# Decode attention on one core: K and V in rows of 64 KiB, four heads in a transfer, three slots

## The chip, the cores and the metric

The kernel runs on 1 core of one Trainium2 chip. The metric is device time in microseconds (us) of that core, as the median of the executions of one kernel.

## The reference

Four sequences decode one token each. Attention with 32 heads reads a cache of 8192 positions; a small feed-forward block reads the same normed input; both are added to x.

```python
B, Sq, D, H, Sk, Dh, F = 4, 1, 512, 32, 8192, 128, 1792      # all bf16
xn = layernorm(x)
q  = (xn @ wq) -> (B, H, 1, Dh)
p  = softmax(q . k_cache * Dh ** -0.5)
o  = p . v_cache
out = x + o.reshape(B, Sq, H*Dh) @ wo + (silu(xn @ w_gate) * (xn @ w_up)) @ w_down
```

K and V are 268 MB each. Everything else is 14 MB: the whole question is how fast 551 MB come in, and whether the work on them hides beneath.

## The kernel before

One tile is two heads of one sequence: 4 MiB of K or of V, on 128 partitions with 32 KiB each, so one DMA row is 32 KiB. Five slots of this size take K and V in turn.

```python
HT = 2                      # heads in a tile
NT = 64                     # tiles
NSLOT = 5; LP = 2           # slots; P*V runs two tiles behind

def t_piece(n, g):          # VectorE: one eighth of a K tile, transposed in pairs of d
    kt = kt_pool.tile([P, TG * Dh], bf16)                      # 5 buffers
    nc.vector.transpose(out=kt..., in_=k_tiles[n][:, g*w:(g+1)*w])   # 128 x 1024 uint32

def s_piece(n, g):          # TensorE: its scores, 4 matmuls
    for jp in range(4):
        mm(s_ps[gr], zq[gr % 2][:, bb, jp, off:off+P], kt[:, jp//2, :, jp%2])

for i in range(NT + LP):
    load_k(i + 2); load_v(i)
    for g in range(8):
        t_piece(i, g); s_piece(i, g)
        if g == 0 and bb == 0: pt_turn(gr - 1)   # VectorE: turns P of the group of two tiles, 2 transposes
    ...                                          # every second tile: maximum, exp (ScalarE), new q
    for k in range(32): pv_chunk(i - LP, k)      # TensorE: P*V of an earlier tile
    row_sums(...)                                # matmul, then VectorE's reciprocal
```
(The set-up, the feed-forward block, the finish of the output and the product with wo are cut.)

## Time and profile before

| | before |
|---|---|
| median (4 runs beside the changed kernel) | 1289.14 us, 1288.77 to 1289.36 |
| span of the profiled run | 1287.1 us |
| last packet of V landed | 1282.4 us |
| VectorE's instructions | 951 |

The lines that show what bounds it stand in the prediction. Here are five more from the page: the busy time of the engines (us, share of the span, number of instructions), two small rows of the list of DMA queues (packets, MB, share of the 16 engines' time), the chain that ended last (followed back from the last instruction), by engine, and the group of the large transposes.

```profile
PE 1083.1 (84%) x4778; PEld 430.3 (33%) x4778; DVE 738.1 (57%) x951; ACT 39.7 (3%) x87; POOL 5.3 (0%) x13
...
q8 instruction: 37, 0.61, 0.2%
q14 instruction: 12, 0.10, 0.0%
...
DMA 50%; PE 31%; DVE 14%; issue 5%; ACT 1%; SPq 0%; DVEq 0%
...
L277 DVE STREAM_TRANSPOSE kt<-slot 128x1024 uint32<-128x1024 uint32 x512 | 587.6, 1210 | 90.4 <-DMA slot<-in_A_k_cache_dram 89.5
```

Half of the chain is DMA: the transfers set the end. The rows q8 and q14, 49 packets with 0.7 MB out of 551, are the engines' instruction fetches.

### The profile page before, as it was taken

The page shows a single profiled execution, that of the slowest core. Times are in us where ns is not written, and L with a number is a line of the kernel's source. Part 1 is how long each engine was busy: PE and PEld are TensorE (multiplying, and loading weights), DVE is VectorE, ACT ScalarE, POOL GpSimd, SP SyncE. Part 2 cuts the span into 40 slices and gives each one's busy share as a digit, 9 for nine tenths or more (in the row PEclk, how much of TensorE's full clock was granted, in tenths as well). Part 3 has the DMA queues.
Part 4 walks back from the last instruction along what each step waited for, and adds up shares of the span by engine and source line. Part 5 has one row for each costly group of instructions (what it writes and reads, how often), then busy time and mean ns, then how long its engine had stood idle before and what let it go on. Part 6 is the DMA issues. An engine that isn't in the chain of part 4 may idle for free.

```text
span 1287.1 us, 11189 instructions
## 1 busy us (share of the span) xinstructions
PE 1083.1 (84%) x4778; PEld 430.3 (33%) x4778; DVE 738.1 (57%) x951; ACT 39.7 (3%) x87; POOL 5.3 (0%) x13
## 2 busy tenths in 40 slices
PE   4888888888888798897997888888887988978788
PEld 1334333333333333332333333333333333333334
DVE  6663556546556556466556566465465465573544
ACT  1000000000000000000000000000000000000000
POOL 1000000000000000000000000000000000000000
PEclk9898898998989999898998989989899898989899
DMA  9999999999999999999999999999999999999997
GB/s 407 427 430 435 437 425 437 429 436 431 432 435 428 436 432 433 431 432 435 431 435 428 434 432 431 436 431 433 430 434 431 437 430 432 433 431 427 433 434 304
DMA packets 21529, 551.49 MB, mean 428 GB/s; under 512 B 2268, under 2 KB 2792, under 8 KB 3944
## 3 DMA queue, kind: packets, MB, share of 16 engines
q1 hardware_dynamic: 21464, 550.78, 99.4%
q8 instruction: 37, 0.61, 0.2%
q14 instruction: 12, 0.10, 0.0%
q10 hardware_dynamic: 16, 0.01, 0.0%
HBM read 550.77 MB, written 0.00 MB: 428 GB/s over the span
## 4 chain that ended last, share of the span: by engine, by line
DMA 50%; PE 31%; DVE 14%; issue 5%; ACT 1%; SPq 0%; DVEq 0%
DMA slot<-in_A_k_cache_dram 44%; PE oacc L76 17%; PE sps L76 12%; DVE kt L277 11%; DMA slot<-in_A_v_cache_dram 6%; PE mps L76 1%; DVE ptz L318 1%; DVE o L356 1%; PE xps L76 1%; DVE o_sb L354 1%; ACT o_sb L353 0%; PE mps L299 0%; DVE otn L377 0%; PE yo_ps L76 0%; DVE rcp L328 0%
## 5 line engine op out<-in xcount | busy, mean ns | idle before, releaser
L76 PE MATMUL sps<-kt,zq 128*128 128x512 bf16 x2048 | 578.3, 421 | 145.2 <-DVE kt L277 128.7
L277 DVE STREAM_TRANSPOSE kt<-slot 128x1024 uint32<-128x1024 uint32 x512 | 587.6, 1210 | 90.4 <-DMA slot<-in_A_k_cache_dram 89.5
L76 PE MATMUL oacc<-slot,ptz 128*8 128x512 bf16 x2016 | 450.4, 379 | 0.4 <-DMA slot<-in_A_v_cache_dram 0.4
L76 PEld LDWEIGHTS <-zq 128*128 128x128 bf16 x2048 | 212.0, 104 | 496.1 <-issue 317.0
L76 PEld LDWEIGHTS <-ptz 128*8 128x8 bf16 x2016 | 177.5, 92 | 258.1 <-issue 27.8
L328 DVE RECIPROCAL rcp<-mps 128x4 f32<-128x4 f32 x32 | 5.9, 183 | 281.9 <-PE mps L76 281.9
L354 DVE TENSOR_TENSOR o_sb<-o_sb,rowu 128x512 f32<-128x512 f32 x16 | 11.1, 693 | 89.2 <-ACT o_sb L353 89.0
L76 PE MATMUL xps<-rowy,o 128*32 128x4 f32 (+1 forms) x228 | 13.5, 205 | 37.3 <-DVE o L356 37.3
L293 DVE TENSOR_REDUCE mx<-sps 128x1 f32<-128x512 f32 x32 | 22.1, 692 | 18.5 <-PE sps L76 18.5
L76 PEld LDWEIGHTS xps<-rowy,o 128*32 128x32 f32 (+1 forms) x228 | 12.1, 154 | 44.9 <-DVE o L356 44.9
L268 DVE COPY zq<-qt 32x8 bf16<-32x8 bf16 x128 | 21.3, 166 | 1.3
L302 DVE TENSOR_REDUCE nm<-mps 128x4 f32<-128x64 f32 x32 | 7.2, 225 | 24.0 <-PE mps L299 24.0
L356 DVE TENSOR_REDUCE o<-o_sb 128x128 f32<-128x512 f32 x16 | 16.3, 1020 | 0.5
L76 PEld LDWEIGHTS mps<-rowb,rs 128*128 128x128 f32 x64 | 9.5, 186 | 13.8 <-issue 13.8
L76 PEld LDWEIGHTS <-slot 128*128 128x128 bf16 x272 | 11.7, 126 | 3.5 <-DVE slot L188 2.6
L76 PE MATMUL mps<-rowb,rs 128*128 128x4 f32 x64 | 12.3, 263 | 0.0
L353 ACT COPY o_sb<-oacc 128x512 f32<-128x512 f32 x16 | 9.4, 586 | 76.8 <-PE oacc L76 76.8
L377 DVE TENSOR_TENSOR otn<-xps,rcp 32x16 bf16<-32x16 f32 x28 | 4.8, 170 | 11.7 <-PE xps L76 10.3
L299 PE MATMUL mps<-ident_f,mx 128*128 128x128 f32 x32 | 10.3, 323 | 0.8 <-DVE mx L293 0.8
L299 PEld LDWEIGHTS mps<-ident_f,mx 128*128 128x128 f32 x32 | 4.3, 133 | 14.7 <-DVE mx L293 14.2
L170 PE MATMUL xps<-ident,kt 4*128 4x4 bf16 x4 | 0.3, 173 | 10.1 <-DVE kt L165 10.1
L76 PE MATMUL yo_ps<-slot,otn 128*4 128x256 bf16 x64 | 8.2, 281 | 0.3 <-DVE otn L366 0.3
(150 smaller groups left out, 148.5 us busy)
## 6 DMA issues: line engine op xcount, KB each, us to landing
slot<-in_A_k_cache_dram SPq DMA_DIRECT2D x64, 4096.0 KB, 39.2
slot<-in_A_v_cache_dram SPq DMA_DIRECT2D x62, 4096.0 KB, 36.8
slot<-in_A_v_cache_dram SPq DMA_DIRECT2D x7, 1024.0 KB, 22.3
slot<-in_A_wq_dram SPq DMA_DIRECT2D x1, 4096.0 KB, 12.3
slot<-in_A_wo_dram SPq DMA_DIRECT2D x1, 3584.0 KB, 40.2
slot<-in_B_w_gate_dram SPq DMA_DIRECT2D x1, 1792.0 KB, 31.9
slot<-in_B_w_up_dram SPq DMA_DIRECT2D x1, 1792.0 KB, 35.8
slot<-in_B_w_down_dram SPq DMA_DIRECT2D x1, 1792.0 KB, 30.9
```

The lines of the kernel that those rows point to most:

```text
L76: nc.tensor.matmul(out_ap, lhsT=lhsT, rhs=rhs, start=start, stop=True, skip_group_check=True, **kw)
L268: nc.vector.tensor_copy(out=zq[gr % 2][a * QB:(a + 1) * QB, :, :, XO + a * QB].rearrange("p b (j r) -> p r j b", r=2), in_=qt[a * QB:(a + ...
L277: nc.vector.transpose(out=kt[:].bitcast(dt.uint32).rearrange("p (j t r) -> p t j r", j=2, r=QB), in_=src.rearrange("p (t j r) -> p t j r", ...
L293: nc.vector.reduce_max(out=mx[:], in_=s_ps[gr][:], axis=AX.X)
L299: nc.tensor.matmul(mps[:, 0:P], lhsT=nmx.pop(gr)[:, 0:1].to_broadcast([P, P]), rhs=ident_f[:, :], is_transpose=True, start=True, stop=True ...
L302: nc.vector.tensor_reduce(out=nm[:], in_=by_row(mps[:, 0:P]), axis=AX.XY, op=ALU.max, negate=True)
L318: nc.vector.transpose(out=t_[y * HP:(y + 1) * HP, :, y, :, :].rearrange("p s u x -> p s (u x)"), in_=p_[y * HP:(y + 1) * HP, :].rearrange( ...
L328: nc.vector.reciprocal(out=rcp[j][:, :, 2 * bp:2 * bp + 2], in_=mps[:, P:P + B].rearrange("p (y b) -> p y b", y=HT))
L353: nc.scalar.copy(out=o_sb[:].rearrange("p u d -> p (u d)"), in_=o_acc[j % 2][:])
L354: nc.vector.tensor_tensor(out=o_sb[:], in0=o_sb[:], in1=rowu[:].unsqueeze(2).to_broadcast([P, NV, Dh]), op=ALU.mult)
L356: nc.vector.reduce_sum(out=o1[:], in_=o_sb[:].rearrange("p u d -> p d u"), axis=AX.X)
L377: nc.vector.tensor_tensor(out=otn[q0:q1, blk * 4:blk * 4 + 4, :], in0=xps[q0:q1], in1=r_[q0:q1, y, :].unsqueeze(1).to_broadcast([QB, 4, B] ...
```

## The change

The intent is to make each transfer larger. A tile becomes four heads, 8 MiB, in rows of 64 KiB; there are half as many tiles, and the turn "transpose K, then multiply the V before it" comes half as often. Memory pays for it: three slots instead of five, three transpose buffers of half the size instead of five, single buffers for P and q, and P*V one tile behind instead of two. Because a buffer now holds half as much, a piece of K is transposed in two halves, one for each group of 32 pairs of d. In before, four matmuls used one transpose; now two do.

```diff
-    HT = 2
+    HT = 4
-    NSLOT = 5
-    LP = 2
+    NSLOT = 3
-    kt_pool = ctx.enter_context(tc.tile_pool(name="ktp", bufs=5))
-    pp = ctx.enter_context(tc.tile_pool(name="pp", bufs=2))
+    kt_pool = ctx.enter_context(tc.tile_pool(name="ktp", bufs=3))
+    pp = ctx.enter_context(tc.tile_pool(name="pp", bufs=1))
 ... (q, identity, residual and feed-forward weights moved into fewer buffers)
-    def t_piece(n, g):
+    def t_piece(n, g, jb):
         w = TG * Dh
-        kt = kt_pool.tile([P, w], dt.bfloat16, name="kt")
-        src = k_tiles[n][:, g * w:(g + 1) * w].bitcast(dt.uint32)
-        nc.vector.transpose(out=kt[:].bitcast(dt.uint32).rearrange("p (j t r) -> p t j r", j=2, r=QB),
-                            in_=src.rearrange("p (t j r) -> p t j r", j=2, r=QB))
+        kt = kt_pool.tile([P, w // 2], dt.bfloat16, name="kt")
+        src = k_tiles[n][:, g * w:(g + 1) * w].bitcast(dt.uint32).rearrange("p (t j r) -> p t j r", j=2, r=QB)
+        nc.vector.transpose(out=kt[:].bitcast(dt.uint32).rearrange("p (t r) -> p t r", r=QB), in_=src[:, :, jb, :])
 ... (s_piece: two matmuls; pt_turn: four transposes of 32 partitions, not two of 64)
+    build_q(0)
+    load_v(0)
+    for i in range(NT):
+        for g in range(NTG):
+            for jb in range(2):
+                t_piece(i, g, jb)
+                s_piece(i, g, jb)
+            if g == 1 and i > 0:
+                pt_turn(i - 1)
+        ... load_v(i), into the slot that this K leaves (i = 30: wo first)
+        max_1(i)
+        for k in range(NK):
+            pv_chunk(i - 1, k)
+            if k == 8:
+                max_2(i)
+        row_sums(i)
+        ... load_k(i + 2), into the slot that this V leaves
+    ... the products with wo of all heads are held back to the end
```

## The prediction

> **What bounds the kernel now.** I read the page first: the slices, the chain, the DMA part. Then the waits of the DMA queue and of the engines, the windows, and the timeline of one cycle in the middle. From the page:
>
> ```profile
> DMA  9999999999999999999999999999999999999997
> GB/s 407 427 430 435 437 425 437 429 436 431 432 435 428 436 432 433 431 432 435 431 435 428 434 432 431 436 431 433 430 434 431 437 430 432 433 431 427 433 434 304
> ...
> q1 hardware_dynamic: 21464, 550.78, 99.4%
> ...
> slot<-in_A_k_cache_dram SPq DMA_DIRECT2D x64, 4096.0 KB, 39.2
> ```
>
> The DMA engines work in every slice but the last, and one queue alone fills 99.4% of their time. A K transfer lands 39.2 us after its issue, though 4 MiB take 9.7 us: about four transfers stand in line, so the five slots keep the queue full. Now the waits, and the windows (sum and mean left out):
>
> ```profile
> DVE rcp L328 <- PE mps L76: 281.9, 32, 9.9
> DVE kt L277 <- DMA slot<-in_A_k_cache_dram: 89.5, 25, 15.9
> ...
> 400.00:800.00 400.00, 341.13 (x1426) 133.21 (x1426) 231.50 (x298) 11.49 (x27) 0.00 (x0) 0.94 1.00 433
> ```
>
> VectorE waits 89.5 us in all for K to land, so transfers set the pace; but the slack is only 89.5 / 32 = 2.8 us for each 8 MiB of K. VectorE also sits idle 281.9 us at one reciprocal, 32 times, until the matmuls of a V tile are over: transposing and P*V take turns. The rate in the middle is 433 GB/s. The timeline shows one turn each:
>
> ```profile
> 448.10 1.38 DVE L318 STREAM_TRANSPOSE ptz<-p__2437 64x512 bf16<-64x512 bf16 x2
> 449.50 8.00 DVE L277 STREAM_TRANSPOSE kt<-slot 128x1024 uint32<-128x1024 uint32 x7
> 450.80 8.55 PE L76 MATMUL sps<-kt,zq 128*128 128x512 bf16 x28 [0.82 <-DVE kt L277]
> 459.28 7.08 PE L76 MATMUL oacc<-slot,ptz 128*8 128x512 bf16 x32
> 466.29 0.38 PE L76 MATMUL mps<-rowb,rs 128*128 128x4 f32 x2
> 466.71 0.18 DVE L328 RECIPROCAL rcp<-mps 128x4 f32<-128x4 f32 x1 [9.21 <-PE mps L76]
> 466.81 9.11 DVE L277 STREAM_TRANSPOSE kt<-slot 128x1024 uint32<-128x1024 uint32 x8
> ```
>
> **What the Trainium skill says.** (1) "DMA: Bandwidth & Descriptors", section "Where 436 GB/s comes from": the SBUF ports cap transfers at 435.2 GB/s. The 433 GB/s here agree: 0.5% is left. (2) Same page, "Why small descriptors are slow (HBM only)": about 3 cycles of overhead for each packet. The packet records agree in size: 32 KiB packets start 1.209 us apart on one engine, against 1.205 us at 27.2 GB/s, so 4 ns each. (3) "VectorE: DVE Perf Modes", "The TRN2 errata": a fixed cost per instruction, 58 cycles (60 ns) in its table. Transposes of 1024 elements start 1.126 us apart, 1.067 us being elements at 0.96 GHz: 59 ns, which agrees. (4) "TensorE: Matmul & The Clock Gate"[...]: gaps over about 3 us halve the clock. Here half clock follows the gaps between phases, and the mean is 0.933.
>
> **The change, part by part.**
>
> Transfers. Rows go from 32 to 64 KiB. K and V before, apart from the last two V tiles, are 126 transfers of 8 packets per engine, 1008; after, about half as many carry these bytes. 504 x 4 ns = 2.0 us, with 63 fewer completions at some 6 ns, 0.4 us: about 2.5 us saved, if a 64 KiB row goes as one packet. An 8 MiB transfer should take 19.35 us, so K and V together set a transfer period of 38.7 us. The last V piece landed at 1282.7 before and the end came 4.4 us later; 2.5 us less gives a transfer floor of about 1284 us of span.
>
> Transposes. Each of 512 becomes two of half the size: 533 + 59 = 592 ns apart. One 8 MiB tile needs 32 x 0.592 + 0.13 = 19.1 us, where 16 x 1.126 = 18.0 stood. This adds 1.0 us per 8 MiB, on the compute path. The three transpose buffers of half size should do: PE needs 2 x 0.22 us for each.
>
> Turning P. Four transposes of 32 partitions instead of two of 64, of the same free size: those stood 0.674 and 0.705 us apart, so 4 x 0.69 = 2.8 us, 1.4 us more.
>
> Phases. With four heads in a tile the turn "transpose K, multiply the V before it" happens once per 8 MiB, not twice. In order of instructions VectorE now has the reciprocal of the row sums ahead of every tile, so nothing of the next K is transposed beside the P*V matmuls. Phase A, VectorE: 19.1 + 2.8 = 21.9. Its last score matmuls and the handover: four took 1.05 us, two 0.6. Phase B, PE: 64 P*V matmuls x 0.219 = 14.0, and 0.4 for the maximum in their midst. Row sums to the next transpose: 0.5 (466.29 to 466.81). Sum 37.4. Every fourth tile ends with the output's finish, 3.6 us before (443.3 to 446.9), about 4.7 now with twice its small matmuls, in place of the 0.5: 1.05 on average. So 38.45 us at full clock. Half clock hits mostly the start of phase A, where PE has room; I estimate 0.4. Compute period 38.85, against 38.7 for the transfers: the two are equal within my error. Before, the same chain was 38.8 - 2.8 = 36.
>
> Slots. Three of 8 MiB: one being transposed or multiplied, one landing or landed, one behind it in line. V follows when K is transposed, K when V is multiplied; each has about one transfer's time, 19.35 us, as lead. Phase A (21.9) is longer than one transfer and B (14.9) shorter, so the lead suffices only if the sum stays under 38.7.
>
> Ends. First K lands at 2.2 + 9.7 + 19.35 = 31.2. A without a P to turn, 19.1, and its softmax, 4.2: 54.5. A, B and handover of tile 1, 37.4: 91.9. Feed-forward, 14.4 before (101.2 to 115.6), partly at half clock and followed by adds that the change drops: estimate 10.5, so tile 2 starts at 102.5. Tiles 2 to 31 take 30 x 38.85 = 1165.5: 1268. Then 56 matmuls with wo, held back to the end, at 0.133 us: 7.4; half of the last V, 32 matmuls, 7.0; finish 2.9; the remaining small matmuls 1.4 + 0.3; last wo 1.1; copy and output 0.8 + 2.3. Sum 23.2, giving 1291 us of span. Device time was 2 us over the span in the run before, so about 1293; without the half-clock cost the transfers rule and it is some 6 us less. I predict 1291.
>
> Freed bookkeeping (residual by matmul, one FFN slot, single buffers for P and q) changes nothing that the path waits for: each is read in the phase before it is rewritten.
>
> **Rivals.**
> R1, transfers still rule. For it: 99.4% now; 38.45 is below 38.7; all issues would have a lead. Then 1284 of span, 1286 of time, less than 0.3% won, since ports leave only 0.5%. Against: half clock, and a tail with held-back wo.
> R2, small transposes do not overlap. The two bf16 ones of 512 elements stood 0.674 us apart, not 0.592. Were the new ones as slow, 32 x 0.08 = 2.6 us would come on each tile: period 41.4, time near 1365, 6% slower. Against: those change their partitions between instructions and the big ones on all partitions do overlap, by 0.076 us.
> R3, three buffers starve VectorE at half clock: PE then needs 0.86 us per piece against 0.59. At 0.3 us lost for each us, beyond some 4 us that the buffers absorb, a window of 6.8 us costs 0.8 and one of 10.2 costs 1.9. At 1 us more per tile, 30 us in all: 1320.
> R4, bigger packets are much faster. The ports' limit speaks against it: all 551.5 MB at 435.2 GB/s take 1267 us.
>
> **Range and chances.** The floor of R1 gives the low end, 1283. Each 0.1 us of period beyond 38.7 costs 3 us, so the upper side is wide: my period is good to 0.6 us, up to 1312. R2 and a strong R3 together get 15%. Faster by over 2% would need 1263, under the ports' limit: 1%. So faster 0.01, within 2% 0.84, slower 0.15.
>
> **What would show it right or wrong.** Right: packets halve to about 13,000; windows in the middle at 432 to 434 GB/s; kt transposes about 0.67 us long and 0.59 apart; VectorE waits for K nearly gone; VectorE's wait at the reciprocal up to some 13 us, 31 times; few DMA gaps, near the end. Wrong: pieces spaced 0.65 us or more, VectorE waiting for PE within phase A, slices under 425 GB/s in the middle (then compute rules, and the time exceeds 1310), or VectorE still waiting for K on most tiles (then R1).

## The result

The changed kernel takes 1303.87 us (median of 4 runs, 1302.94 to 1307.31) against 1289.14 before. The ratio is 1.0119, with a 95% interval from 1.01 to 1.0139; ratios here are the mean time of one kernel's runs over the mean of the other's in the same rounds, so not quite the ratio of the medians. The change costs 14.7 us. The prediction said 1291, with a range up to 1312: the class and the range held, the point was 12.9 us too low. The profiled run was the slowest of the four (1307.31 us, span 1305.5). The four order by their granted clock, 0.922, 0.926, 0.931 and 0.933 for 1307.31, 1304.74, 1302.99 and 1302.94 us: a first hint that TensorE's clock has come to matter.

The page of the changed kernel, the lines that answer to those of before:

```profile
PE 1136.1 (87%) x4725; PEld 463.8 (36%) x4788; DVE 807.9 (62%) x1509; ACT 35.0 (3%) x79; POOL 3.6 (0%) x11
...
GB/s 418 418 432 438 432 432 436 428 442 420 446 422 442 428 436 430 436 430 434 432 436 427 428 424 438 424 432 432 414 436 432 430 428 424 436 436 406 409 339 227
DMA packets 12466, 551.56 MB, mean 422 GB/s; under 512 B 1260, under 2 KB 1784, under 8 KB 3064
...
q8 instruction: 37, 0.61, 0.2%
q14 instruction: 21, 0.17, 0.0%
...
PE 58%; DVE 20%; issue 18%; DMA 2%; ACT 0%; DVEq 0%; SPq 0%
...
L272 DVE STREAM_TRANSPOSE kt<-slot 128x512 uint32<-128x512 uint32 x1024 | 629.5, 678 | 32.8 <-DMA slot<-in_A_k_cache_dram 12.5
```

Packets have fallen to 12,466. DMA has left the chain (2%), and VectorE waits 12.5 us for K where it waited 89.5. VectorE has 558 instructions more, and q14 21 fetches in place of 12. The last four slices sag to 406, 409, 339 and 227 GB/s. The timeline of one turn in the middle (start, duration, engine, what; in brackets the idle time before and who ended it):

```profile
618.02 2.46 DVE L272 STREAM_TRANSPOSE kt<-slot 128x512 uint32<-128x512 uint32 x4
618.76 0.39 PE L75 MATMUL sps<-kt,zq 128*128 128x512 bf16 x1 [0.87 <-DVE kt L272]
619.35 1.80 PE L75 MATMUL sps<-kt,zq 128*128 128x512 bf16 x6 [0.20 <-DVE kt L272]
620.41 2.81 DVE L309 STREAM_TRANSPOSE ptz<-p__3628 32x512 bf16<-32x512 bf16 x4
623.25 17.53 DVE L272 STREAM_TRANSPOSE kt<-slot 128x512 uint32<-128x512 uint32 x28
624.01 13.64 PE L75 MATMUL sps<-kt,zq 128*128 128x512 bf16 x43 [2.86 <-DVE kt L272]
637.86 3.58 PE L75 MATMUL sps<-kt,zq 128*128 128x512 bf16 x12 [0.21 <-DVE kt L272]
```

The four transposes that turn P stand in one block of 2.81 us, and TensorE has nothing to do for 2.86 us. The records of the granted clock show half clock (0.5) from 625.20 to 628.61, soon after. During it VectorE's pieces come 0.84 us apart instead of 0.593, because three buffers make it wait for TensorE: 28 pieces take 17.53 us, where 28 x 0.593 is 16.6.

The packet records of the trace show the transfers' side. They carry no number of the DMA engine, but each packet can be followed to the one that starts where it ends. In the changed kernel:

| from one landing of 8 MiB to the next | us | how often (120 to 1242 us) |
|---|---|---|
| no fetch of q14 in between | 19.30 | 37 of 58 |
| a fetch of q14 in between, VectorE's with few exceptions | 20.28 (median) | 20 of 58 |
| 2 x 4 MiB in before, no fetch of q14 | 2 x 9.67 = 19.34 | |

(One more took 19.72 without a fetch. Fetches of q8 fall into both rows.)

A fetch of 8 KiB at 367.60 us took 0.31 us, and the 64 KiB packet that follows it 3.03 us where 2.42 is the rule, 0.92 us together. The landings show 0.97 us: so much does one DMA engine of sixteen lose with each fetch. The spread between the first and the last engine to finish a transfer grows with each of VectorE's fetches, 2.4 us at 125 us, 4.3 at 320, 7.9 at 594; the few fetches of other engines in q14 leave it as it is. Followed from packet to packet, all nine of VectorE's fetches in before lie in one chain, the one that finishes last; in the changed kernel the ten from 118 to 715 us do (later the queue runs dry at times, and the chains can't be told apart). The fetches of q8 go round eight other chains. So VectorE's fetches all fall on the same DMA engine, and a tile has landed only when that engine is done.

VectorE has a fetch for every 128 of its instructions, the separate wait instructions included. Before, it ran 951 plus some 230 waits, nine blocks; after, 1509 plus some 930, nineteen. I read the growth of the waits from the program, no run tests it: with three buffers most transposes wait for both VectorE's own earlier work and TensorE.

The theory after this reading: the doubled fetches hold the transfers to 2 x 19.30 + 0.97 x 17 / 28.5 = 39.2 us for each pair of K and V (17 of VectorE's fetches fall in the 28.5 pairs from 124 to 1242 us), instead of the predicted 38.7. The rivals: compute sets the pace (half clock, the order of the turn, the late start), or rows of 64 KiB with three slots cannot do 38.7 in any case.

### The profile page after: what moved, and what is told of

It is laid out like the page before. It is cut to its first block, busy times and chain, and to the rows that moved or that the text cites. A ratio compares the mean times of both kernels' runs of the same rounds, so it can differ in the third digit from the quotient of the medians. Undisturbed runs are those within 1.5% of the kernel's fastest.

```text
span 1305.5 us, 12271 instructions
## 1 busy us (share of the span) xinstructions
PE 1136.1 (87%) x4725; PEld 463.8 (36%) x4788; DVE 807.9 (62%) x1509; ACT 35.0 (3%) x79; POOL 3.6 (0%) x11
## 2 busy tenths in 40 slices
DMA packets 12466, 551.56 MB, mean 422 GB/s; under 512 B 1260, under 2 KB 1784, under 8 KB 3064
## 4 chain that ended last, share of the span: by engine, by line
PE 58%; DVE 20%; issue 18%; DMA 2%; ACT 0%; DVEq 0%; SPq 0%
PE oacc L75 34%; PE sps L75 21%; DVE kt L272 14%; DVE ptz L309 5%; DMA slot<-in_A_k_cache_dram 2%; PE mps L75 1%; PE yo_ps L75 1%; PE xps L75 1%; DVE o L346 1%; PE mps L291 1%; DVE kt L344 0%; ACT kt L343 0%; DVE rcp L319 0%; DVE otn L366 0%; ACT p__385 L300 0%
## 5 line engine op out<-in xcount | busy, mean ns | idle before, releaser
L75 PE MATMUL sps<-kt,zq 128*128 128x512 bf16 x1985 | 635.4, 430 | 133.3 <-DVE kt L272 133.0
L272 DVE STREAM_TRANSPOSE kt<-slot 128x512 uint32<-128x512 uint32 x1024 | 629.5, 678 | 32.8 <-DMA slot<-in_A_k_cache_dram 12.5
L75 PE MATMUL oacc<-slot,ptz 128*16 128x512 bf16 x2016 | 446.9, 380 | 0.0
L75 PEld LDWEIGHTS <-ptz 128*16 128x16 bf16 x2016 | 206.6, 105 | 226.9 <-issue 13.7
L319 DVE RECIPROCAL rcp<-mps 128x4 f32<-128x4 f32 x32 | 5.9, 185 | 363.9 <-PE mps L75 363.9
L285 DVE TENSOR_REDUCE mx<-sps 128x1 f32<-128x512 f32 x32 | 22.1, 692 | 22.4 <-PE sps L75 22.4
L75 PE MATMUL xps<-rowy,o 128*32 128x4 f32 (+1 forms) x226 | 10.5, 204 | 15.3 <-DVE o L346 15.3
L263 DVE COPY zq<-qt 32x4 bf16<-32x4 bf16 x128 | 21.1, 165 | 1.3
L75 PEld LDWEIGHTS mps<-rowb,rs 128*128 128x128 f32 x64 | 9.7, 190 | 14.9 <-issue 12.9
L75 PE MATMUL mps<-rowb,rs 128*128 128x4 f32 x64 | 12.5, 266 | 1.7 <-ACT p__385 L300 1.7
L75 PEld LDWEIGHTS <-slot 128*128 128x128 bf16 (+1 forms) x274 | 11.7, 123 | 6.3 <-DVE slot L191 2.6
L344 DVE TENSOR_TENSOR kt<-kt,rowu 128x512 f32<-128x512 f32 x8 | 5.5, 693 | 11.2 <-ACT kt L343 10.4
L291 PEld LDWEIGHTS mps<-ident_f,mx 128*128 128x128 f32 x32 | 4.3, 133 | 14.2 <-issue 12.9
L346 DVE TENSOR_REDUCE o<-kt 128x128 f32<-128x512 f32 x8 | 8.2, 1022 | 0.3
L343 ACT COPY kt<-oacc 128x512 f32<-128x512 f32 x8 | 4.7, 586 | 96.8 <-PE oacc L75 96.8
L75 PE MATMUL yo_ps<-slot,kt 128*4 128x256 bf16 x28 | 5.8, 402 | 1.6 <-DVE kt L235 1.6
## 6 DMA issues: line engine op xcount, KB each, us to landing
slot<-in_A_v_cache_dram SPq DMA_DIRECT2D x5, 2048.0 KB, 16.4
```

The source lines that it names most:

```text
L75: nc.tensor.matmul(out_ap, lhsT=lhsT, rhs=rhs, start=start, stop=True, skip_group_check=True, **kw)
L263: nc.vector.tensor_copy(out=zq[a * QB:(a + 1) * QB, :, XO + a * QB].rearrange("p (j r) -> p r j", r=2), in_=qt[a * QB:(a + 1) * QB, half, ...
L272: nc.vector.transpose(out=kt[:].bitcast(dt.uint32).rearrange("p (t r) -> p t r", r=QB), in_=src[:, :, jb, :])
L285: nc.vector.reduce_max(out=mx[:], in_=s_ps[n][:], axis=AX.X)
L291: nc.tensor.matmul(mps[:, 0:P], lhsT=nmx.pop(n)[:, 0:1].to_broadcast([P, P]), rhs=ident_f[:, :], is_transpose=True, start=True, stop=True, ...
L319: nc.vector.reciprocal(out=rcp[j][:, :, b], in_=mps[:, P:P + HT])
```

## The experiments

All runs are right, unless said otherwise. In the same rounds before took 1288.94 us (first four runs), 1288.77 (next four) and 1289.22 (last four).

### One suspected cost of compute at a time

**Spread the turns of P** over four groups, so that TensorE has no gap of 2.9 us.

```diff
-            if g == 1 and i > 0:
-                pt_turn(i - 1)
+            if 1 <= g <= HT and i > 0:
+                pt_turn(i - 1, range(g - 1, g))
```

> The four transposes that turn P, which stand in a row after the first four K pieces, are dealt out one by one after K pieces 4, 6, 8 and 10. Same instructions, same VectorE work. Theory (compute cycle sets the time; PE's 2.9 us gap at the turn brings half clock some us later, and VectorE then starves behind three buffers): half-clock windows become fewer, the K pieces at 0.84 us spacing vanish in most tiles, 0.5 to 0.9 us less per tile, in all 15 to 18 us, ending near the transfers' limit: 1285 to 1292 us, mean clock above 0.95. Rival (three slots or 8 MiB transfers make the loss in the transfers): no change, 1303 +- 3.

Measured: 1301.59 us (1300.93 to 1301.84), ratio 1.0097.

**Fill the gap** with ten matmuls that nobody reads, to hold the clock.

```diff
                 pt_turn(i - 1)
+                d_ps = psX.tile([P, 512], dt.float32, name="xps")
+                for _ in range(10):
+                    mm(d_ps[:], zq[:, 0, 0:P], k_tiles[i][:, 0:512], start=True)
```

> Ten idle matmuls (K times q into a spare PSUM tile, never read) fill PE's gap at the turn of P; nothing else moves. If the half clock is the cause, as much is won as by dealing the turn out (1285 to 1292 us), though PE does more work. If in a1 it were the order on VectorE that helped and not the clock, this run stays at 1303 +- 3.

Measured: 1301.38 us (1301.15 to 1301.52), ratio 1.0096. The windows from 400 to 800 us of the changed kernel, of spread and of filled, in this order (busy us of PE, weight loads, VectorE, ScalarE, GpSimd; then the granted clock, DMA share, GB/s):

```profile
400.00:800.00 400.00, 356.02 (x1386) 141.86 (x1406) 255.68 (x479) 8.96 (x22) 0.00 (x0) 0.93 1.00 431
```
```profile
400.00:800.00 400.00, 356.24 (x1419) 139.96 (x1419) 251.02 (x475) 9.74 (x24) 0.00 (x0) 0.97 1.00 433
```
```profile
400.00:800.00 400.00, 374.36 (x1521) 149.08 (x1520) 247.99 (x475) 9.73 (x24) 0.00 (x0) 0.98 1.00 433
```

Both edits do what they should: the clock rises to 0.97 and 0.98 (half clock stands for 114 and 98 us of the whole run, 204 in the changed kernel), and the score phase (TensorE's first to last score matmul of a tile, mean of 14 tiles) falls from 22.86 us to 22.36 and 22.00. That is 0.5 to 0.9 us for each of 32 tiles, 16 to 27 us. Only 2.3 and 2.5 came out. The waits and the chain by engine say where the rest went; of spread:

```profile
DVE kt L272 <- DMA slot<-in_A_k_cache_dram: 21.7, 10, 11.4
```
```profile
PE 56%; DMA 24%; DVE 17%; issue 3%; ACT 0%; SPq 0%; DVEq 0%
```

DMA is back in the chain with 24% (27% in filled), and VectorE waits for K again: after 362 us seven times in spread and eleven in filled, 7.7 and 16.3 us, where the changed kernel has no such wait any more. Their turn is 39.23 and 39.19 us (twelve tiles from 695 us). Compute did get faster, and ran into the transfers, which stood right behind.

**Start each K earlier**, beside P*V: the row sums come after the second group of the next tile.

```diff
+            if g == 1 and i > 2:
+                row_sums(i - 1)
             if g == 1 and i > 0:
                 pt_turn(i - 1)
...
-        row_sums(i)
+        if i == 1:
+            row_sums(i)
```

> The row sums of a tile and their reciprocal are moved behind the first four K pieces of the next tile, so VectorE can transpose three pieces of the next K beside the P*V matmuls (three buffers hold them). Theory: the cycle gets shorter by three pieces and the handover, 1.8 to 2.3 us per tile, so its sum falls to about 37 us, under the 38.7 us of transfers, and the transfers rule: 1284 to 1290 us, VectorE's wait for PE at the reciprocal gone, waits for K to land return. Rival (transfers rule already): 1303 +- 3.

Measured: 1306.37 us (1306.05 to 1306.99), ratio 1.0135, a miss. VectorE transposes three pieces ahead and then waits for TensorE; TensorE uses these up at once and then has a gap of 3.75 us at the turn of P (776.6 to 780.4 us), so its score phase grows to 23.86 us. What the start gains, the phase loses.

**Load the first K in four parts**, so that the first tile starts sooner.

```diff
-    load_k(0)
+    load_k(0, (64,) * 4)
```

> The first K comes in four transfers of 2 MiB, so tile 0 can be transposed while it lands and tile 1 starts when its K has landed, some 5 to 6 us sooner. Theory (a chain of compute from start to end): the whole chain moves, 5 to 6 us less, 1297 to 1299 us. Rival (transfers set the time): no change.

Measured: 1304.19 us (1302.88 to 1304.75), ratio 1.0117: the same as the changed kernel. TensorE starts tile 2 4.7 us before the profiled run of the changed kernel (105.5, not 110.2). By tile 8 the lead is 3.1 us (P*V starts at 362.4, not 365.5), and spread and filled are at the same point (362.0). VectorE waits for K 17.2 us in all, 16.4 of it before this point, so part of the lead is eaten by the transfers. The rest is still there at tile 28 (1166.1, not 1169.8). The median shows nothing of it, but the profiled run of the changed kernel was 3.4 us over its own median: what became of the lead is not shown.

So four edits of compute move the time by -2.5 to +2.5 us. The two that make the score phase shorter meet the same pace, that of the transfers.

### The suspected cost of the fetches, doubled

Each reciprocal is preceded by 48 tiny writes on VectorE, 1536 in all, one column each, in the 11 us in which VectorE waits for P*V anyway. This adds twelve blocks of 128 instructions and next to no work on the path.

```diff
             rcp[j] = small.tile([P, HT, B], dt.float32, name="rcp")
+        for c in range(48):
+            nc.vector.memset(pad_t[:, c:c + 1], 0.0)
         nc.vector.reciprocal(out=rcp[j][:, :, b], in_=mps[:, P:P + HT])
```

In the changed kernel:

> 48 one-column memsets on VectorE before each tile's reciprocal, where it waits 11.7 us for PE anyway: 1536 instructions more (some 12 more instruction fetches of 8 KiB), no data, no wait of PE longer. Theory now (the transfers set the pace through the one DMA engine that also fetches VectorE's instructions; each fetch cost it 0.31 us and the packet beside it 0.6 us more): 12 x 0.9, 10 to 11 us more, 1313 to 1315 us, the gap between the first and the last DMA engine still about 8 us. Rival (compute cycle sets the pace): the memsets lie in an idle wait, so 1303 +- 3.

In the kernel before:

> The same 48 memsets per reciprocal in the kernel before, which has 9.9 us of idle wait there and four transfers in line. Theory: the fetches add to one DMA engine's work whatever the depth of the queue: 12 x 0.84, 9 to 10 us more, 1297 to 1300 us. Rivals (compute, or a queue too shallow in the new kernel alone): 1289 unchanged.

Measured: 1313.58 us (1312.73 to 1314.01), 9.7 us over the changed kernel (measured in other rounds, between which before differs by 0.4 us); and 1299.33 us (1299.21 to 1299.49), 10.6 us over before. The rows of the queue, first of the changed kernel with the writes, then of before with them:

```profile
q14 instruction: 33, 0.27, 0.0%
```
```profile
q14 instruction: 24, 0.20, 0.0%
```

Twelve more fetches in each, at 0.97 us: 11.6 us expected by the measured unit, 9.7 and 10.6 found. VectorE still waits for P*V 333.7 us at the reciprocal (363.9 without the writes), so its own time had room. The last K lands at 1252.3 us instead of 1241.9. In before, transfers land every 9.66 us with no fetch between them and 10.63 with one: the same 0.97. Twelve packets that the page rounds to 0.0% of the DMA time are worth 0.7 to 0.8% of the kernel in either version.

### Fewer fetches

**Transposes of the old size in the changed kernel.** Two buffers of 4 KiB replace three of 2 KiB (room comes from q kept in PSUM and small tiles merged). VectorE has 996 instructions.

```diff
-    kt_pool = ctx.enter_context(tc.tile_pool(name="ktp", bufs=3))
+    kt_pool = ctx.enter_context(tc.tile_pool(name="ktp", bufs=2))
-                t_piece(i, g, jb)
+                if jb == 0:
+                    t_piece(i, g)
                 s_piece(i, g, jb)
 ... (t_piece writes both groups of d, as before; room made elsewhere)
```

> The new kernel with whole transposes (1024 elements) in two buffers of 4 KiB; the room comes from q kept in PSUM and the two output halves in one PSUM bank. 513 transposes fewer and half the extra waits: about 11 instruction fetches instead of 19. Theory: transfers lose 8 x 0.9 = 7 us, but two buffers starve VectorE at half clock (1.75 us of matmuls per piece against 1.13), so compute may become the bound at about 39 us per tile: 1296 to 1301 us. If fetches do not matter: no gain or a loss, 1303 to 1310.

Measured: 1308.78 us (1307.35 to 1310.44), ratio 1.0156, a miss. The waits show why:

```profile
PE sps L75 <- DVE kt L268: 184.5, 260, 14.2
```

TensorE waits 184.5 us for transposes (133.0 in the changed kernel). With two buffers VectorE stands still until TensorE has used one up. Fewer fetches were bought with a slower phase.

**Spread and early together, with the products with wo moved into the last tile's transposing.**

```diff
                 s_piece(i, g, jb)
+                if i == NT - 1 and g >= 2:
+                    wo_some(1)
 ... (and the edits of spread and of early)
```

> The new kernel with the turn of P dealt out, the row sums late and the wo matmuls put into the last tile's transposing (some 6 us off the tail): compute has slack everywhere, instructions as many as before. Theory: the steady part does not get faster (39.2 us per tile, transfers with fetches), only the tail and the empty queue near the end do: 1293 to 1298 us. If compute were the bound: 1285 to 1289.

Measured: 1309.9 us (1308.52 to 1312.14), ratio 1.016, a miss of my own making: wo had not landed when the first of its products came up, and TensorE stood still for 2.8 us; the products between the scores then stretch the phase. The last score phase takes 32.4 us, 22.4 in spread. Up to there it tells something: VectorE waits 218.5 us for K, 24 times, yet the P*V of tile 29 ends at 1241.2 us, no sooner than in spread (1240.0). Slack in compute is not speed.

**Old size, spread and early together**, without the moved wo: the slack that the two buffers lacked.

```diff
 ... (the edits of "transposes of the old size", of spread and of early)
```

> The changed kernel with transposes of the size of before (two buffers of 4 KiB in place of three of 2 KiB), the turns of P spread over four groups, and the row sums moved behind the third and fourth transpose so that VectorE starts the next K beside P*V. VectorE has 998 instructions and 404 second waits, 1402 in all, 11 blocks of 128, against 19 in the changed kernel. Fetch theory: 8 fetches fewer at 0.9 us, 7 us less than the order with spread turns (1301.6), so about 1294 to 1296, as long as two buffers do not starve VectorE as they did without the early start (39.5 us a tile there). Rival (the pace is set by compute in every variant of three slots): 1301 to 1309.

Measured: 1307.89 us (1306.15 to 1308.9), ratio 1.0144. As an expectation of the time this failed by 12 us; the rival's 1301 to 1309 held. But it separates the two limits. VectorE has ten fetches in the steady part instead of 18, and the last K lands at 1235.9 us: 4.7 us sooner than in spread (1240.6), 6.0 sooner than in the changed kernel (1241.9). The timeline there:

```profile
1234.77 10.52 PE L75 MATMUL oacc<-slot,ptz 128*16 128x512 bf16 x48
1235.95 2.37 DVE L268 STREAM_TRANSPOSE kt<-slot 128x1024 uint32<-128x1024 uint32 x2 [2.00 <-DMA slot<-in_A_k_cache_dram]
1245.22 1.98 PE L75 MATMUL sps<-kt,zq 128*128 128x512 bf16 x8
```

K is there at 1235.95, but TensorE multiplies V until 1245.2. Its score phases take 23.2 us, 24.9 in every fourth tile, and the turn 39.27 us (twelve tiles from 697.5 to 1168.7). Now compute is the limit and the transfers wait for it: the chain has 2% of DMA again.

```profile
PE 46%; DVE 39%; issue 12%; DMA 2%; ACT 0%; SPq 0%; DVEq 0%
```

The fetch theory told the landing in kind; that the time would follow was wrong, since this variant's compute is as slow as the pace it was to leave. Of the 7 us expected, 0.06 us on each undisturbed landing went another way: they are 19.35 us apart here and in the other kernel with transposes of the old size, 19.30 in those with halves. Over 57 landings this is 3 us, and I have no cause for it.

**Larger transposes in the kernel before**: five for each K tile, not eight, and the 128 small copies of q moved to ScalarE. If fetches cost so much, before should gain too.

```diff
-            for g in range(NTG):
-                t_piece(i, g)
-                s_piece(i, g)
+            for g, m in ((0, 1), (1, 2), (3, 2), (5, 2), (7, 1)):
+                t_piece(i, g, m)
+                s_piece(i, g, m)
-            nc.vector.tensor_copy(
+            nc.scalar.copy(
                 out=zq[gr % 2]...
```

> The kernel before, rows of 32 KiB and five slots, with five transposes for each K tile instead of eight (1, 2, 2, 2 and 1 groups; three buffers of 8 KiB) and the 128 small copies of q moved from VectorE to ScalarE. VectorE has 633 instructions and 166 second waits, 799 in all, 6.2 blocks of 128 against 9.3 before. Fetch theory: 3 fetches fewer at 0.84 us on the engine that finishes last, 2 to 2.5 us less than before: about 1287. Rival (fetches do not matter; VectorE's saved time is hidden anyway): 1289, the same as before, or slower by larger pieces.

Measured: 1291.08 us (1289.87 to 1291.86), ratio 1.0014: a miss, if anything slower. Its row of the queue:

```profile
q14 instruction: 10, 0.08, 0.0%
```

Ten, not nine: ScalarE's copies seem to have brought a fetch of ScalarE's own (it has 258 instructions and waits, 126 in before). And the gain of VectorE's fewer fetches has little room: in before, the DMA engine that finishes last is 7.84 us behind the first, and the one before it 7.56. Speeding up the last one can win 0.3 us before another is last. The packets show which: behind the engine with VectorE's nine fetches come those that serve q8, with four or five fetches of 16 KiB each. In this run both stand at 7.5 and 7.4, and the last packet lands at 1281.9 us (1282.4 before); the tail after it grew by 1.5 us. Adding fetches to the slowest engine cost 9.7 and 10.6 of 11.6 us here; taking them away can pay only down to the next slowest, which fits this run.

### The transfers alone

All work on K and V is left out, and the result is wrong: only the loads remain, three slots of 8 MiB or five of 4.

```diff
-    build_q(0)
-    ... (the whole loop)
+    load_v(0)
+    for i in range(1, NT):
+        if i > 1:
+            load_k(i)
+        load_v(i)
```

> The changed kernel with all work on K and V left out: wq, the first norm and the projection of q stay, then only the 64 transfers of 8 MiB, each waiting only for its slot's previous transfer. Wrong result on purpose. VectorE has a few dozen instructions, so next to no instruction fetches of its queue. Theory (the transfers themselves keep the predicted pace, the fetches lengthen it): every landing 19.30 us after the one before, 64 x 19.30 + 9.7 for wq + about 5 at the ends = 1250 us, with no engine of the sixteen falling behind by more than 3 us. Rival (64 KiB rows, or the depth of three slots, cannot hold 38.7 us per pair of K and V in any case): 19.6 us each as in the changed kernel, 1270 us.

> The kernel before with the same cut: only the 128 transfers of 4 MiB, five slots. Wrong result on purpose. Theory: 9.67 us each, 128 x 9.67 + 9.7 + 5 = 1252.5 us, so 2 to 3 us over the loads with 64 KiB rows. Rival (larger rows gain nothing): equal within 0.5 us.

Measured: 1253.04 us (1252.87 to 1253.48) with rows of 64 KiB, 1255.07 (1255.04 to 1255.17) with 32. The windows from 200 to 1200 us, 64 KiB first:

```profile
200.00:1200.00 1000.00, 0.00 (x0) 0.00 (x0) 0.00 (x0) 0.00 (x0) 0.00 (x0) 1.00 1.00 434
```
```profile
200.00:1200.00 1000.00, 0.00 (x0) 0.00 (x0) 0.00 (x0) 0.00 (x0) 0.00 (x0) 0.50 1.00 433
```

The larger rows win 2.0 us, as the packets promised. Transfers land 19.32 us apart: three slots and 64 KiB rows do hold 38.64 us for a pair. Both totals are 3 us over what I had expected: 1.7 and 1.5 us of it because all landings are on average 19.33 and 9.682 us apart, the rest because my allowance for the ends was short. The rival "64 KiB or three slots can't do it" falls for the transfers by themselves.

## Why the prediction was right or wrong

The class and the range held, and most of the single steps. Packets: predicted about 13,000, found 12,466, and 2.0 us won in the loads alone. Pieces 0.592 us apart: 0.593. Turning P 2.8 us: 2.81. P*V with the maximum 14.4: 14.37. From the first transpose of the last tile to the end, 60.6 by the prediction's terms (37.4 + 23.2): 59.4 in the profile (1246.1 to 1305.5). R2 fell with the spacing of the pieces, R4 with the 19.30 us of an undisturbed landing. One of its signs of being wrong did come: six slices from the third to the 36th are under 425 GB/s, the lowest 414, and the middle (400 to 800 us) ran at 431, not 432 to 434. Compute ruled, as it said for this case, though under 1310 us.

**The step that failed is "Compute period 38.85, against 38.7 for the transfers".** Both terms were too small, by almost the same amount.

| us for one tile (a pair of K and V) | predicted | changed kernel | what was missed |
|---|---|---|---|
| compute | 38.85 | 39.25 (twelve tiles, 698.8 to 1169.8) | half clock costs 0.86, not 0.4 |
| transfers | 38.7 | 39.2 (2 x 19.30 + 0.58) | VectorE's fetches doubled |

In the profiled run the account is this. The prediction's sum gave 1291.2 us of span; 1305.5 was measured, 14.3 more. Of it 10.0 are the pace (29 turns of 39.19 us from tile 2 to tile 31, not 38.85), 7.7 the start, and -3.4 the tail (58.7 from TensorE's first matmul of tile 31, 38.85 + 23.2 in the sum). That the tail hid a part of the error is luck.

**Compute.** "Half clock hits mostly the start of phase A, where PE has room; I estimate 0.4." In three tiles of four it hits after the block of four P transposes, which itself makes the gap, and in the middle of the phase, where three buffers let TensorE's slowness through to VectorE; in every fourth, after the finish of the output, it begins before the tile's first matmul (696.9 and 698.8 us) and lasts 10.24 us. R3 named the mechanism, with a size of 0.8 to 1.9 us. Its size is the 0.86 us by which the score phase shrank when the gap was filled. The gap was 2.86 us, less than the some 3 us that the prediction cites as the limit.

**Transfers.** R1's floor took the transfers of before and subtracted the packets' gain. It did not ask what else the DMA engines carry. The Trainium skill's page "Runtime: NRT & Kernel Launch", "Instruction fetch mechanics", says that a sequencer fetches its instructions by a DMA queue of its own and calls the cost of crossing a block "mostly hidden". Here it isn't hidden where the transfers rule: 0.97 us each, 18 times from 60 us on, against 8 times in before, where it already was part of the time.

**Why either alone would have given nearly this time.** The two limits are within 0.1 us of each other. Take the half clock away and the transfers rule (spread and filled: -2.3 and -2.5 us). Take fetches away with a compute that is no faster, and compute rules (old size with spread and early: the last K 6.0 us sooner, no gain of time). What neither limit explains is the end. With spread, whose parts are easiest to add up because the transfers rule to the last K, the spans differ by 12.0 us (1299.1 against 1287.1):

| from before to spread | us |
|---|---|
| last packet lands at 1289.4, not 1282.4 | +7.0 |
| of it by working: 10 more fetches of VectorE x 0.97 | +9.7 |
| and 58 landings x (19.34 - 19.30) | -2.3 |
| from the last packet to the end: 9.7, not 4.7 | +5.0 |

The last row is order. In before, TensorE waits for the last piece of V and has only a few matmuls after it. In the changed kernel the last K is followed by 21 MB (wo and two tiles of V), 48 us of transfers at 434 GB/s, but by 58 us of work: scores of tile 31, P*V of 30, the products with wo, P*V of 31. That end hangs on the landing of the last K, not of the last V. The timeline of the changed kernel's end shows it:

```profile
1271.73 12.06 PE L75 MATMUL oacc<-slot,ptz 128*16 128x512 bf16 x55
1284.04 5.95 PE L75 MATMUL yo_ps<-slot,otn 128*4 128x256 bf16 x53
1290.17 6.64 PE L75 MATMUL oacc<-slot,ptz 128*16 128x512 bf16 x30
1296.74 2.25 PE L75 MATMUL xps<-ptz,slot 128*128 128x4 bf16 x80
```

The last packet is in at 1292.0, and TensorE is still on the first half of the last V. The prediction had this tail nearly right; it had the last K too early. The same place in before:

```profile
1280.81 1.42 PE L76 MATMUL xps<-ptz,slot 128*128 128x2 bf16 x48
1282.71 0.59 PE L76 MATMUL xps<-ptz,slot 128*128 128x2 bf16 x16 [0.48 <-DMA slot<-in_A_v_cache_dram]
```

From spread to the changed kernel itself are 2.3 us more by the medians, the part of compute that shows.

**The start** was predicted too early as well: TensorE began tile 2 at 110.2 us, not 102.5. Tile 1 ended at 95.4, not 91.9, and the feed-forward block took 14.8 us, not 10.5, ten of them at half clock. The run with the first K in parts took 4.7 us of this back and won nothing by the median, so what the late start costs is not settled.

**What stays open.** No run had both a compute of some 38.4 us and few fetches, so what the changed form could reach with both is not shown. That VectorE's fetches meet the same DMA engine is read from packets that follow each other, as the trace doesn't number the engines; past 715 us of the changed kernel only the spacing of the landings speaks for it. The 0.06 us by which undisturbed landings differ with the size of the transposes has no cause. No complete version tried beats the kernel before.

## What to carry to other kernels

When transfers fill the DMA engines, count the instructions of every engine before and after a change, waits included: here an instruction that ran 512 times was halved in size, and with the waits that fewer buffers added, VectorE's fetches past the data doubled from nine to nineteen. Look for the limit that stands second before expecting a gain from removing the first; here the two were 0.1 us apart, and the two repairs of the clock returned 2.3 and 2.5 us of the 16 to 27 that they freed. And in the last tiles compare the work after each landing with the transfers after it: the end may hang on an earlier landing than the last.

## What the Trainium skill lacked or had wrong

- "Runtime: NRT & Kernel Launch", "Instruction fetch mechanics", has blocks of 16 KiB (256 instructions) and a cost "mostly hidden". In these traces VectorE's fetches are 8 KiB for 128 instructions, and those of q8, TensorE's by their number (some 9,500 instructions in 37), 16 KiB (0.61 MB). Where the transfers rule, each of VectorE's costs 0.97 us of the landing on which it falls (20.27 against 19.30 us); twelve more cost 9.7 and 10.6 us.
- "DMA: Bandwidth & Descriptors", "Queues, rings and completion order", lists the refill among what runs in row 14, but no page says that one engine's fetches fall on one of the sixteen DMA engines, so that the slowest engine and not the mean rate decides when a transfer lands. In before all nine of VectorE's lie in one chain of packets, while those of 16 KiB go round eight others. The spread between first and last engine grew from 2.4 us (125 us into the run) to 7.9 (594 us) while the windows still showed 431 GB/s and full DMA share.
- "TensorE: Matmul & The Clock Gate", "Why this matters for your kernels", warns of gaps over about 3 us. Here a gap of 2.86 us was followed, in the same tile, by 3.41 us at half clock, and filling it won back 0.86 us of each score phase.
